# Merging two column-nesting subtractions into one, and four output planes of a unit into one addition

## The chip, the cores and the metric

The kernel runs on one core of one Trainium2 chip. The metric is the device time of one execution in microseconds (us). Engines are named as in the profile: PE (TensorE matmuls), PEld (weight loads), DVE (VectorE), ACT (ScalarE), POOL (GpSimd), SP (SyncE, which issues most DMAs).

## The reference, cut to what matters

```python
B, C, HW, E = 2, 512, 64, 1152           # bf16 in, bf16 out
def reference(x, t_emb, g1, be1, w1, w_emb, g2, be2, w2):
    h = conv3(_silu(gn(x, g1, be1)), w1)      # group norm, SiLU, 3x3 convolution
    emb = _silu(t_emb) @ w_emb
    h = h + emb.reshape(B, C, 1, 1)
    h = conv3(_silu(gn(h, g2, be2)), w2)
    return x + h
```

Both 3x3 convolutions run as a scheme that saves multiplications over rows: DVE makes combinations of input rows ("planes"), PE multiplies them, ACT moves the products out of PSUM, the memory that matmuls write to, with a scale (an "evacuation"), and DVE combines them into four output planes. From the second of the eight chunks on, columns are nested in the same way.

## The kernel before: the parts that matter

The work is cut into 32 "units" (8 chunks times 4 output channel tiles; the last unit has code of its own). The kernel holds nearly all of SBUF in one tile, the "arena", and places everything in it by hand:

```python
    VB = [o, o + 16640 + 2240 + 14848]        # column planes, two chunks
    Z = o + 16640 + 2240
    ...
    AB = [o, o + AF];  o += 2 * AF            # two input buffers; SiLU works in place in them
    YS = [o, o + YF];  o += 2 * YF            # two output buffers
    MB = o;            o += 4 * MS            # M: four planes of 512
    ...
    SD0 = Z + 10016                           # S: first layer
    O0 = [Z + 11552, Z + 12592, Z + 13632]    # o planes of the first layer
    SD1 = Z + 12768                           # S: second layer
    ar = pool.tile([P, NA], F16, name="ar")   # the arena
```

Every operation goes into the kernel's own planner with a modelled cost and with the exact set of elements that it reads and writes. The planner makes one order for each engine and then issues the program in that order. The tile framework, not the planner, decides afterwards which semaphores (signals that another engine or a DMA queue is done) each instruction waits for, from the program's order and from the access patterns.

```python
    def tt(out, a, b, op, name=""):
        pl.op("DVE", 0.075 + 0.000521 * out.n, lambda: nc.vector.tensor_tensor(out=out.ap, in0=a.ap, in1=b.ap, op=op),
              regs(a, b), regs(out), name)
```

A unit ends so, with `M(i)` at `MB + 512 i`:

```python
        tt(tw(SD, 512), M(0, 2), M(2, 2), AD, nm + "s")
        tt(M(0, 2), M(2, 2), M(0, 2), SB_, nm + "d")
        scal(se[0], M(2), M(1), 8.0, nm + "8")            # on ACT or DVE, by a table
        scal(se[1], M(3), M(1), 2.0, nm + "2")
        scal(se[2], A(SD + 1024, [[1, 512]]), A(SD + 512, [[1, 512]]), 4.0, nm + "4")
        yr = lambda r0: A(ys + r0 * RW, [[RW, 16], [33, 2], [1, 32]])
        tt(yr(0), A(MB, [[0, 2], [1, 512]]), A(MB + 1024, [[512, 2], [1, 512]]), AD, nm + "y")
        tt(yr(16), A(SD, [[0, 2], [1, 512]]), A(SD + 1024, [[-512, 2], [1, 512]]), AD, nm + "y")
```

The first addition (the "first" or M half below) reads M alone and needs two scaled planes, the second (the S half) reads S alone and needs one. The nesting (28 times) is four subtractions or additions over a small buffer X:

```python
        X = lambda i: A(xb + i, [[RW, 8 * nf], [1, 32]])
        for kind, (i, j, op) in enumerate(((32, 33, SB_), (1, 0, SB_), (33, 0, SB_), (33, 0, AD))):
            tt(A(vnest(c, ct, kind, 0), [[1, 256 * nf]]), X(i), X(j), op, nm)
```

## Time and profile before

| | before |
|---|---|
| median of the first 3 runs | 476.97 us (476.17 to 478.6) |
| span of the profiled run | 474.9 us |
| first matmul starts | 4.5 us |
| 2936 matmuls, each at the median spacing of its shape | 455.3 us |
| stalls of over 0.4 us between matmuls, in sum | 4.8 us |
| smaller excess between matmuls, in sum | 5.4 us |
| after the last matmul, itself counted at its median, to the end | 4.9 us |

The last five rows add up to the span. They are worked out from the start times of successive matmuls in the trace: the median distance is 222 ns for 512 columns and 109 ns for 256, and what exceeds the median of its shape is a stall. PE works at its pace nearly all the time.

The page of the kernel before: its line of busy times (with shares of the span and instruction counts), then busy tenths in 40 equal slices, and PE's granted clock in tenths.

```profile
PE 461.3 (97%) x2936; PEld 283.4 (60%) x2936; DVE 428.2 (90%) x847; ACT 371.9 (78%) x580; POOL 38.8 (8%) x66
...
PE   6998999899999999999999999999999999999995
...
DVE  1699999999999999988999999998999999996447
...
PEclk9998999999999999999999999999999999999999
```

Busy time of each engine in three stretches (the columns stand in the first line); PE is full in two of them.

```profile
core 0: us, PE busy (x) PEld busy (x) DVE busy (x) ACT busy (x) POOL busy (x), PEclk, DMA share, GB/s
80.00:100.00 20.00, 18.28 (x91) 8.76 (x90) 19.93 (x42) 17.87 (x40) 0.00 (x0) 1.00 0.43 142
180.00:200.00 20.00, 20.00 (x116) 11.14 (x114) 19.76 (x41) 14.66 (x33) 2.05 (x4) 1.00 0.62 201
290.00:310.00 20.00, 20.00 (x149) 14.35 (x148) 19.86 (x33) 16.84 (x20) 2.74 (x4) 1.00 0.67 171
```

DVE's groups by shape: count, busy us, mean ns of one, and idle time of DVE just before them with what ended it. The 15 additions of 2048 elements belong to another step (adding S onto M).

```profile
L328 DVE TENSOR_TENSOR ar<-ar 128x1024 f16<-128x1024 f16 x272 | 179.1, 692 | 11.4 <-ACT ar L351 10.7
...
L328 DVE TENSOR_TENSOR ar<-ar 128x512 f16<-128x512 f16 x78 | 31.1, 428 | 0.1
L328 DVE TENSOR_TENSOR ar<-ar 128x2048 f16<-128x2048 f16 x15 | 18.3, 1219 | 7.0 <-ACT ar L351 7.0
```

Who waited for whom, in us in total, times, and the longest:

```profile
ACT ar L351 <- DVE ar L328: 34.8, 35, 3.2
DVE ar L328 <- ACT ar L351: 24.2, 17, 3.8
...
PE psum L379 <- ACT ar L351: 1.7, 1, 1.7
...
PE psum L379 <- DVE fs L441: 1.2, 2, 0.9
```

PE itself waits little once it has started: beside these two entries there is one wait of 1.3 us for DVE, at 36 us.

### The profile page before, as it was taken

To read this page: it belongs to the slowest core of one execution; us is meant where nothing else is said; L and a number is where in the kernel's file an instruction comes from. 1 tells how busy PE (TensorE), PEld (TensorE's weight loads), DVE (VectorE), ACT (ScalarE), POOL (GpSimd) and SP (SyncE) were. 2 spreads that over 40 slices of the span, in tenths; PEclk is the share of its full clock that TensorE was granted. 3 is DMA by queue.
4 is the path that set the end of the run, shared out by engine and by line. 5 is a ranking of instruction groups with operands and counts; after the bars stand their busy time and mean duration, and the time that the engine had idled before them with its cause. 6 is when DMAs were issued, how large, how long until landed. Compare 5 with 4: busy or idle time off the path is not lost.

```text
span 474.9 us, 8229 instructions
## 1 busy us (share of the span) xinstructions
PE 461.3 (97%) x2936; PEld 283.4 (60%) x2936; DVE 428.2 (90%) x847; ACT 371.9 (78%) x580; POOL 38.8 (8%) x66
## 2 busy tenths in 40 slices
PE   6998999899999999999999999999999999999995
PEld 5753555455555545555555576666666666677783
DVE  1699999999999999988999999998999999996447
ACT  5878999899999777689988778768776788655452
POOL 4100000010000000100000001104011111111111
PEclk9998999999999999999999999999999999999999
DMA  8943566366252466664775886685778487366534
GB/s 326 373 160 109 159 203 190 96 223 219 94 172 77 179 187 201 184 235 159 253 259 197 290 273 214 166 225 135 200 184 227 100 251 190 117 128 138 112 46 90
DMA packets 40505, 87.18 MB, mean 184 GB/s; under 512 B 6416, under 2 KB 14480, under 8 KB 40464
## 3 DMA queue, kind: packets, MB, share of 16 engines
q1 hardware_dynamic: 35520, 77.60, 48.5%
q0 software_dynamic: 4656, 9.05, 12.3%
q8 instruction: 23, 0.38, 0.3%
q14 instruction: 18, 0.15, 0.1%
q10 hardware_dynamic: 288, 0.01, 0.0%
HBM read 62.25 MB, written 31.32 MB: 197 GB/s over the span
## 4 chain that ended last, share of the span: by engine, by line
PE 40%; DVE 24%; ACT 7%; issue 4%; POOL 0%; DVEq 0%; ACTq 0%; POOLq 0%
PE psum L379 40%; DVE ar L328 22%; ACT ar L351 7%; DVE ar L332 2%; POOL fs L450 0%; POOL ar L364 0%; DVEq L1176 0%; DVE fs L441 0%; DVE fs L914 0%; DVE fs L915 0%; DVE fs L452 0%; DVE fs L917 0%; DVE fs L921 0%; DVEq L328 0%; ACTq L351 0%
## 5 line engine op out<-in xcount | busy, mean ns | idle before, releaser
L379 PE MATMUL psum<-ar 128*128 128x512 f16 (+2 forms) x2729 | 443.7, 325 | 4.3 <-ACT ar L351 1.7
L328 DVE TENSOR_TENSOR ar<-ar 128x1024 f16<-128x1024 f16 (+5 forms) x689 | 404.0, 648 | 27.4 <-ACT ar L351 24.2
L379 PEld LDWEIGHTS <-ar 128*128 128x128 f16 (+1 forms) x2765 | 266.6, 98 | 175.2 <-issue 7.4
L351 ACT ACTIVATE ar<-psum 128x512 f16<-128x512 f32 (+2 forms) x224 | 156.5, 714 | 53.3 <-PE psum L379 44.7
L351 ACT ACTIVATE ar<-ar 128x512 f16<-128x512 f16 (+6 forms) x185 | 158.1, 890 | 31.2 <-DVE ar L328 30.2
L351 ACT ACTIVATE ar<-ar,fs 128x2112 f16<-128x2112 bf16 (+1 forms) x32 | 68.7, 2149 | 6.8 <-DVE fs L454 2.9
L364 POOL DMA_DIRECT2D out_dram<-ar x15 | 18.1, 1207 | 115.9 <-DVE ar L328 91.8
L332 DVE TENSOR_SCALAR ar<-ar 128x512 f16<-128x512 f16 (+2 forms) x73 | 26.4, 381 | 0.5 <-ACT ar L351 0.5
L379 PE MATMUL psum<-ar,ones_bf 128*128 128x260 bf16 x128 | 18.3, 284 | 4.5 <-DMA ar<-in_x_dram 4.5
L351 ACT ACTIVATION_READ_ACCUMULATOR ar<-psum 128x1 f32 x100 | 20.8, 208 | 0.0
L379 PEld LDWEIGHTS <-ones_bf 128*128 128x128 bf16 x128 | 12.6, 100 | 9.9 <-issue 3.2
L450 POOL TENSOR_TENSOR fs<-fs 128x1 f32<-128x1 f32 (+1 forms) x7 | 9.0, 1281 | 108.9 <-DVE fs L448 97.2
L368 POOL MEMSET ar<- 128x65 f16 (+5 forms) x28 | 4.4, 197 | 121.8 <-PE psum L379 29.5
L364 POOL DMA_DIRECT2D ar<-ar x4 | 3.7, 924 | 79.2 <-DVE ar L328 63.8
L351 ACT ACTIVATION_READ_ACCUMULATOR ar<-ar 128x1 f32 x36 | 7.1, 198 | 0.0
L441 DVE COPY fs<-psum 128x2 f32<-128x2 f32 (+1 forms) x7 | 1.1, 158 | 4.7 <-PE psum L379 4.7
L967 DVE SCALAR_TENSOR_TENSOR ar<-psum,ident 128x128 bf16<-128x128 f32 x4 | 1.2, 290 | 4.6 <-PE psum L379 4.6
L379 PEld LDWEIGHTS psum<-fs,ones_neg 128*128 128x128 f32 x36 | 4.6, 191 | 0.8 <-issue 0.3
L379 PE MATMUL psum<-fs,ones_neg 128*128 128x1 f32 (+3 forms) x36 | 4.7, 244 | 0.1
L452 DVE TENSOR_TENSOR fs<-fs 128x1 f32<-128x1 f32 (+1 forms) x7 | 1.1, 157 | 2.2 <-POOL fs L450 2.1
L415 ACT ACTIVATE s_sb<-tparm 128x18 bf16<-128x18 bf16 x1 | 0.2, 218 | 3.1 <-DMA tparm<-in_t_emb_dram 3.1
L410 ACT ACT_TABLE_LOAD x1 | 1.3, 1283 | 1.7 <-PEq L1165 1.7
(40 smaller groups left out, 17.9 us busy)
## 6 DMA issues: line engine op xcount, KB each, us to landing
ar<-in_w_dram SPq DMA_DIRECT2D x32, 384.0 KB, 3.9
ar<-in_x_dram SPq DMA_DIRECT2D x16, 552.5 KB, 3.9
h_scr<-ar SPq DMA_DIRECT2D x16, 520.0 KB, 3.4
ar<-h_scr SPq DMA_DIRECT2D x16, 520.0 KB, 3.9
out_dram<-in_x_dram SPq DMA_DIRECT2D x30, 260.0 KB, 4.7
out_dram<-ar POOLq DMA_DIRECT2D x15, 520.0 KB, 5.8
u_scr<-ar SPq DMA_DIRECT2D x16, 384.0 KB, 2.8
ar<-u_scr SPq DMA_DIRECT2D x4, 1536.0 KB, 7.0
```

What stands on the lines that cost most here:

```text
L328: pl.op("DVE", 0.075 + 0.000521 * out.n, lambda: nc.vector.tensor_tensor(out=out.ap, in0=a.ap, in1=b.ap, op=op), regs(a, b), regs(out), name)
L332: pl.op("DVE", cost or 0.075 + 0.00026 * out.n, lambda: nc.vector.tensor_scalar(out=out.ap, in0=a.ap, scalar1=s, scalar2=None, op0=ALU.mul ...
L351: lambda: nc.scalar.activation(out=out.ap, in_=a.ap, func=func, scale=sc, **kw), regs(*rr), regs(*ww), name)
L364: lambda: eng.dma_start(out=out, in_=in_, **kw), regs(*r), regs(*w), name, lat=3.2 if sw else None, after=after, sw=sw)
L368: pl.op("POOL" if eng == "gpsimd" else "DVE", 0.08 + 0.0005 * out.n, lambda: e.memset(out.ap, v), (), regs(out), name)
L379: nc.tensor.matmul(out.ap, lhsT=lhsT.ap, rhs=rhs.ap, start=st, stop=sp, skip_group_check=True)
L410: nc.scalar.activation(out=fs[:, WARM:WARM + 1], in_=fs[:, WARM + 1:WARM + 2], func=ACT.Silu)
L415: nc.scalar.activation(out=s_sb[:], in_=tparm[:], func=ACT.Silu)
L441: pl.op("DVE", 0.16, lambda: V.tensor_copy(out=F(tot, 2 * n).ap, in_=ps.ap), regs(ps), regs(F(tot, 2 * n)), name)
L450: pl.op("POOL", 0.85, lambda: nc.gpsimd.tensor_tensor(out=F(rs, n).ap, in0=N.ap, in1=F(NEGH, n).ap, op=ALU.pow), regs(N), regs(F(rs, n)), ...
L452: small(lambda: V.tensor_mul(out=S.ap, in0=F(rs, n).ap, in1=F(g, n).ap), [F(rs, n)], [S], name)
L967: pl.op("DVE", 0.3, lambda: nc.vector.scalar_tensor_tensor(out=j2.ap, in0=g.ap, scalar=1.0 / HW, in1=ident[:], op0=ALU.mult, op1=ALU.mult, ...
```

## The change

Intent: fewer DVE instructions for the same elements, 31 in the output additions (all units but the last) and 28 in the nesting, on an engine that is 90% busy. The two scaled planes in M change places so that one pattern can walk all four.

```diff
-        for kind, (i, j, op) in enumerate(((32, 33, SB_), (1, 0, SB_), (33, 0, SB_), (33, 0, AD))):
-            s0 = vnest(c, ct, kind, 0)
-            tt(A(s0, [[1, 256 * nf]]), X(i), X(j), op, nm)
+        X2 = lambda i, j: A(xb + i, [[j - i, 2], [RW, 8 * nf], [1, 32]])
+        tt(A(vnest(c, ct, 0, 0), [[1, 512 * nf]]), X2(32, 1), X2(33, 0), SB_, nm)
+        for kind, op in ((2, SB_), (3, AD)):
+            tt(A(vnest(c, ct, kind, 0), [[1, 256 * nf]]), X(33), X(0), op, nm)
...
-        scal(se[0], M(2), M(1), 8.0, nm + "8")
-        scal(se[1], M(3), M(1), 2.0, nm + "2")
+        scal(se[0], M(3), M(1), 8.0, nm + "8")
+        scal(se[1], M(2), M(1), 2.0, nm + "2")
...
-        yr = lambda r0: A(ys + r0 * RW, [[RW, 16], [33, 2], [1, 32]])
-        tt(yr(0), A(MB, [[0, 2], [1, 512]]), A(MB + 1024, [[512, 2], [1, 512]]), AD, nm + "y")
-        tt(yr(16), A(SD, [[0, 2], [1, 512]]), A(SD + 1024, [[-512, 2], [1, 512]]), AD, nm + "y")
+        tt(A(ys, [[RW, 32], [33, 2], [1, 32]]), A(MB, [[SD - MB, 2], [0, 2], [1, 512]]),
+           A(MB + 1536, [[SD - MB - 512, 2], [-512, 2], [1, 512]]), AD, nm + "y")
```

Between S and M lie the o planes of the first layer, the column planes of every second chunk (`VB[1]`), both input buffers `AB` and both output buffers `YS`.

## The prediction

> **What bounds the kernel now.** TensorE (PE). The page has PE busy 461.3 of 474.9 us (97%), VectorE (DVE) 428.2 (90%), ScalarE (ACT) 371.9. In the table of 20 us stretches PE is busy 20.00 of 20 in most stretches from 40 to 460 us. It is also at its own pace: start to start, successive 512-column matmuls stand 222 ns apart (median of 1247; 90th percentile 224) and 256-column ones 109 ns. With each matmul at its shape's median the 2936 matmuls need about 455.2 us. The rest of the span is 4.5 us before the first, 5.1 us after the last, and about 10 us of PE stalls: 1.4 us at 36 us (waits for DVE), 1.9 us at 90 us (waits for ACT), 1.0 us at 176 and 0.5 us at 289 us (wait for DVE in the second normalisation), and small ones, mostly before 41 us.
>
> DVE is full from 80 to 320 us (19 to 20 of 20), so it looks like a second limit, and the chain of waits that ended last runs along DVE from 114 to 177 us and from 229 to 289 us. But PE loses only about 1 us and 0.5 us where that chain enters PE. In the second layer the chain is PE alone: 1204 matmuls in 168.3 us. In the last unit it returns to DVE, and the change does not touch that unit's outputs.
>
> **What the change removes.** One DVE instruction in each of 31 units (two 1024-element additions become one of 2048), and one in each of 28 nested tiles (two 512-element subtractions become one of 1024 in 12 tiles; two of 1024 become one of 2048 in 16). Elements stay the same. Start to start the trace has 350 ns for a 512-element subtraction of this kind, 634 for one of 1024, 601 for a contiguous addition of 1024 and 1135 for 2048. So a merge saves about 2x601-1135 = 67 ns in a unit, 2x350-634 = 66 in a small tile and (an estimate) 70 to 130 in a large one: together 4 to 5 us, 1% of DVE's busy time. The Trainium skill (Vector Engine (DVE) Microarchitecture Reference, 5.2 Measured stream behaviour) gives about 75 ns per instruction; the trace's 67 agrees.
>
> **What it adds or moves.** The single output addition waits for all three scaled planes, where the first half needed two, and frees the intermediate planes about 0.6 us later. The nest needs nothing new. Zero and negative outer steps keep innermost steps of 1, so I expect the same rate per element. The planned order shifts: statistics matmuls of the second image move among the first units' matmuls, and one normalisation chain moves earlier.
>
> **On the critical path.** Only the part that shortens DVE-caused stalls counts: at most about 1.5 us at 176 and 289 us, likely half; the early stalls lie before any changed instruction. The 1.9 us at 90 us is an ACT matter that the new order may shrink or worsen by 1 to 2 us.
>
> **Prediction.** 475.8 us, 80% range 473.4 to 478.2. Faster by over 2%: 0.02; within 2%: 0.96; slower by over 2%: 0.02.
>
> **What would show the steps.** PE busy and matmul spacing unchanged; 59 fewer DVE instructions; merged additions near 1.22 us each, so DVE busy about 424 us; a little more DVE idle, mostly after 200 us; PE stalls near 176 and 289 us equal or shorter.
>
> **What would make it wrong.** Merged accesses at half rate: each output addition would take about 2.2 us, DVE busy would grow by over 30 us and PE would wait: 10 us or more slower. Or the new order putting a statistics matmul ahead of its data: some us of PE waiting before 100 us.

## The result, and the profile after

The changed kernel took 507.94 us (median of 4 runs, 506.35 to 510.5) against 476.83 us before (4 runs). The ratio is 1.065, with a 95% interval from 1.060 to 1.071: slower by over 6%. Ratios in this text are the mean time of one kernel's fast runs over that of the other's of the same rounds, so they are not quite the ratio of the medians quoted.

The same sum, for the profiled runs (us):

| | before | after |
|---|---|---|
| first matmul starts | 4.5 | 4.5 |
| matmuls at the median spacing of before | 455.3 | 455.3 |
| stalls of over 0.4 us | 4.8 | 27.4 |
| smaller excess | 5.4 | 11.6 |
| after the last matmul | 4.9 | 5.9 |
| span | 474.9 | 504.6 |

So 22.6 of the 29.7 us are new stalls of PE, and 6.2 are smaller excess; 5.0 of these are matmuls that run slowly after a stall, as shown below. The page of the changed kernel, the same lines as before:

```profile
PE 468.2 (93%) x2936; PEld 285.7 (57%) x2936; DVE 427.4 (85%) x788; ACT 370.5 (73%) x580; POOL 38.2 (8%) x66
...
PE   6989995999999939999999968999999998999995
...
DVE  1799959998996796887999899999989989985547
...
PEclk9999998999999988999999987999999999999999
```

DVE has 59 instructions fewer and is busy for 0.8 us less; it isn't slower, it stands idle more. Where it stands idle shows in the groups by shape:

```profile
L328 DVE TENSOR_TENSOR ar<-ar 128x1024 f16<-128x1024 f16 x190 | 126.8, 692 | 10.9 <-ACT ar L351 10.1
L328 DVE TENSOR_TENSOR ar<-ar 128x2048 f16<-128x2048 f16 x62 | 76.3, 1237 | 35.7 <-ACT ar L351 15.6 <-issue 9.9 <-DMA ar<-in_x_dram 8.1
...
L328 DVE TENSOR_TENSOR ar<-ar 128x512 f16<-128x512 f16 x54 | 21.3, 422 | 1.6 <-ACT ar L351 1.6
```

The 62 instructions of 2048 elements are 15 as before, 16 merged nests and 31 merged output additions. They take 1237 ns in the mean, so the full rate is kept: the half rate that the prediction named as its main danger did not come. But DVE now stands idle for 35.7 us ahead of this group. Sorted by operand shape in the trace, 28.9 us of it stand ahead of 21 of the 31 output additions (before: 0.6 us ahead of one). And part of it ended with a DMA from the input `x`, which no output addition needs.

The waits, the same pairs as before, with two new ones:

```profile
ACT ar L351 <- DVE ar L328: 69.7, 41, 5.8
...
DVE ar L328 <- ACT ar L351: 33.2, 28, 3.4
...
PE psum L379 <- ACT ar L351: 15.9, 7, 5.5
DVE ar L328 <- issue: 9.9, 5, 4.2
PE psum L379 <- DVE fs L441: 8.7, 2, 8.6
DVE ar L328 <- DMA ar<-in_x_dram: 8.1, 3, 4.6
```

ACT's waits for DVE doubled. One of PE's new waits, before and after (PE in order of time: start, us, what; in brackets the idle time before it). Before:

```profile
175.06 0.51 PE L379 MATMUL psum<-fs,ones_neg 128*128 128x8 f32 x4
175.42 0.81 PE L379 MATMUL psum<-ar 128*128 128x256 f16 x6
177.10 1.27 PE L379 MATMUL psum<-ar 128*128 128x512 f16 x5 [0.86 <-DVE fs L441]
```

After:

```profile
180.11 0.51 PE L379 MATMUL psum<-fs,ones_neg 128*128 128x8 f32 x4
180.47 1.03 PE L379 MATMUL psum<-ar 128*128 128x256 f16 x8
190.06 1.44 PE L379 MATMUL psum<-ar 128*128 128x512 f16 x3 [8.55 <-DVE fs L441]
```

The same 512-column matmul, after the small matmuls of the second normalisation, waited 0.86 us before and 8.55 us now, both for the DVE copy of the normalisation's sums (L441): DVE reached that copy late. What follows such a stall shows in the same stretches as before, in their number of matmuls and in the granted clock (the column after POOL):

```profile
core 0: us, PE busy (x) PEld busy (x) DVE busy (x) ACT busy (x) POOL busy (x), PEclk, DMA share, GB/s
80.00:100.00 20.00, 14.50 (x61) 6.45 (x61) 19.03 (x39) 16.49 (x33) 0.00 (x0) 0.83 0.47 149
180.00:200.00 20.00, 11.45 (x62) 6.19 (x60) 14.79 (x30) 11.79 (x24) 0.87 (x1) 0.83 0.46 129
290.00:310.00 20.00, 13.22 (x76) 8.47 (x74) 19.93 (x40) 15.36 (x21) 0.31 (x2) 0.74 0.80 283
```

After one stall of 5.7 us, which ends at 85.5 us, and after the one of 8.7 us, successive 512-column matmuls stand about 427 ns apart, 11 and 6 of them, in place of 222. The Trainium skill (TensorE: Matmul & The Clock Gate, "What's actually happening") says that PE falls to half its clock after an idle window of about 3.4 us and needs about as long a busy one to come back; its section "Wait — 56ns, not 53.3ns?" gives 426.7 ns for 512 columns at the half clock. This trace agrees with the 427 ns; slow running begins once after a stall of 2.8 us too (at 299 us). In the kernel before it is found only near 40 us, in seven matmuls, after the stall of 1.4 us at 36 us; its stalls of 0.5 to 1.9 us at 90, 176 and 289 us were not followed by it. So in these traces a stall well under 3.4 us can start it and need not.

What do the output additions wait for? That stands in the built programs, as the list of semaphores ahead of each instruction (DMAHW and DMASW are DMA queues; own numbers dropped). Three of the additions before, and the same units in the changed kernel (here "earlier" is the half that is issued first: S in units 4 and 9, M in unit 18):

```
before   unit 4   earlier: DMAHW6, DVE             later: DVE
before   unit 9   earlier: DMAHW7, ACT             later: DVE, ACT
before   unit 18  earlier: DMASW4, ACT             later: none
after    unit 4   DMAHW6, DMAHW7, DVE, ACT
after    unit 9   DMASW2, DMAHW3, DMAHW4, DVE, ACT, POOL
after    unit 18  DMASW4, DMAHW6, DMAHW7, DVE, ACT, POOL
```

POOL does nothing that an output addition of unit 9 could need: it writes zero rows in `AB` (and raises a power in the normalisation). This gave the theory.

**Theory T, false waits.** The merged access reaches from S to M across some 30,000 elements. The framework appears to take all that lies between as read. So the addition waits for loads, SiLU and evacuations that it doesn't need, and later writers of that stretch wait for it.

**Rival O, the order.** The planner got other entries, so it made another order on each engine, and that order is bad on the chip.

**Rival P, one instruction for two.** The single addition must wait for all three scaled planes, and holds M longer.

### The profile page after: what moved, and what is told of

Same layout as the page of the kernel before. It is cut to its first block, busy times and chain, and to the rows that moved or that the text cites. A ratio compares the mean times of both kernels' runs of the same rounds, so it can differ in the third digit from the quotient of the medians.

```text
span 504.6 us, 8130 instructions
## 1 busy us (share of the span) xinstructions
PE 468.2 (93%) x2936; PEld 285.7 (57%) x2936; DVE 427.4 (85%) x788; ACT 370.5 (73%) x580; POOL 38.2 (8%) x66
## 3 DMA queue, kind: packets, MB, share of 16 engines
q0 software_dynamic: 4656, 9.05, 11.6%
## 5 line engine op out<-in xcount | busy, mean ns | idle before, releaser
L379 PE MATMUL psum<-ar 128*128 128x512 f16 (+2 forms) x2729 | 450.3, 327 | 26.1 <-ACT ar L351 15.9
L328 DVE TENSOR_TENSOR ar<-ar 128x1024 f16<-128x1024 f16 (+6 forms) x630 | 401.9, 693 | 56.8 <-ACT ar L351 33.2
L351 ACT ACTIVATE ar<-ar 128x384 bf16<-128x384 bf16 (+6 forms) x185 | 158.5, 891 | 50.7 <-DVE ar L328 44.3
L364 POOL DMA_DIRECT2D ar<-ar x4 | 3.7, 923 | 85.5 <-ACT ar L351 64.6
L441 DVE COPY fs<-psum 128x2 f32<-128x2 f32 (+1 forms) x7 | 1.1, 159 | 4.7 <-PE psum L379 4.7
```

Source lines behind the costliest of these rows:

```text
L351: lambda: nc.scalar.activation(out=out.ap, in_=a.ap, func=func, scale=sc, **kw), regs(*rr), regs(*ww), name)
L364: lambda: eng.dma_start(out=out, in_=in_, **kw), regs(*r), regs(*w), name, lat=3.2 if sw else None, after=after, sw=sw)
L379: nc.tensor.matmul(out.ap, lhsT=lhsT.ap, rhs=rhs.ap, start=st, stop=sp, skip_group_check=True)
L441: pl.op("DVE", 0.16, lambda: V.tensor_copy(out=F(tot, 2 * n).ap, in_=ps.ap), regs(ps), regs(F(tot, 2 * n)), name)
```

## The experiments

Fifteen kernels ran, all with correct results, each against runs of the kernel before on the same chip (476.2 to 476.9 us in the median).

### y_near: the planes side by side, everything else the same

```diff
-    SD0 = Z + 10016
-    O0 = [Z + 11552, Z + 12592, Z + 13632]
-    SD1 = Z + 12768
+    O0 = [Z + 10016, Z + 11056, Z + 12096]
+    SD0 = SD1 = MB + 4 * MS          # S right behind M; the area Z is shorter by 1664
-    NF = 640
+    NF = 512                         # makes room; the kernel's own assertion says that these columns are unused
```

> The changed kernel with the planes M and SD laid side by side in the arena (nothing else lies between them); all instructions and their order on PE, DVE, ACT and SP are the same as in the changed kernel, as the built programs show; only the semaphore waits differ. Theory T (false waits): the merged output addition reads an access pattern that reaches from SD to M, and whatever lies between these two is taken for read, so the addition waits for loads and evacuations that it doesn't need, and they for it. T: 473 to 478 us, DVE idle ahead of the output additions under 4 us (28.9 in the changed kernel), no PE stall over 2 us after 100 us. Rival O (the planner's new order is bad on the chip): 505 to 511, stalls where they were. Rival P (one addition must wait for all three scaled planes, and holds M longer): 505 to 511 too.

Measured: 479.25 us (4 runs, 478.76 to 480.92), ratio to before 1.0056 (1.0025 to 1.0087). The loss is gone but for some 2.5 us, with the same instructions in the same order on PE, DVE, ACT and SP as in the 507.94 us. Ahead of the group of merged instructions DVE now idles 11.7 us in place of 35.7, and nothing but ACT ends it (mind that the 15 older additions of 2048 have about 6.7 of it; the output additions have 4.9):

```profile
L328 DVE TENSOR_TENSOR ar<-ar 128x1024 f16<-128x1024 f16 x190 | 127.1, 695 | 10.4 <-ACT ar L351 9.7
L328 DVE TENSOR_TENSOR ar<-ar 128x2048 f16<-128x2048 f16 x62 | 76.3, 1238 | 11.7 <-ACT ar L351 11.5
```

The stretches are full or nearly full again, at a clock of 1.00:

```profile
core 0: us, PE busy (x) PEld busy (x) DVE busy (x) ACT busy (x) POOL busy (x), PEclk, DMA share, GB/s
80.00:100.00 20.00, 18.65 (x93) 8.79 (x91) 19.85 (x39) 17.18 (x40) 0.00 (x0) 1.00 0.47 148
180.00:200.00 20.00, 20.00 (x116) 11.16 (x115) 19.86 (x39) 14.15 (x33) 1.18 (x3) 1.00 0.70 196
290.00:310.00 20.00, 18.68 (x134) 13.09 (x134) 19.91 (x32) 16.61 (x20) 3.32 (x5) 1.00 0.65 163
```

The waits in the built program are back to real ones: unit 4 waits for DMAHW6 and DVE, unit 9 for DVE and ACT, unit 18 for DMASW4, DVE and ACT. Matmul for matmul (the order on PE is the same), the changed kernel falls behind y_near by 7, 9 and 9 us near 82, 178 and 283 us, all in the first layer, and by some 4.5 us after 370 us. Rivals O and P, which both said 505 to 511, fall as the explanation of the 28 us. DVE's idle time ahead of the output additions fell by 24.0 us, the time by 28.7; how much of that comes from the additions' own waits, and how much from later writers that wait for them, was not separated. The expected 473 to 478 was missed by 1.3 us, and the 4 us of idle time by 0.9: something small is left. (No PE stall over 2 us after 100 us was expected; the longest is 1.8 us.)

### y_two_narrow: the changed plan, issued as two narrow instructions

The plan keeps its one entry of 2048 elements; only the issue differs:

```diff
-            nc.vector.tensor_tensor(out=<4 planes>, in0=<M and S>, in1=<M and S>, op=AD)
+            nc.vector.tensor_tensor(out=<planes 0, 1>, in0=<M>, in1=<M>, op=AD)
+            nc.vector.tensor_tensor(out=<planes 2, 3>, in0=<S>, in1=<S>, op=AD)
```

> The changed kernel, planned exactly as it is (one entry of 2048 elements in the plan), but the output addition issued as two instructions back to back, planes 0 and 1 from M, planes 2 and 3 from SD, as before. T: 474 to 479 us, no false waits, DVE pays about 67 ns more per unit. O: 505 to 511, for the order is that of the changed kernel. P: some 476 to 500, for the first half still sits where the plan put the whole.

Measured: 479.59 us (479.26 to 481.43), ratio 1.0065 (1.0033 to 1.0096), 0.6 us over the range. In the old arena, with the changed kernel's order, no wide access means no loss but for some 2.7 us, much as in y_near. Both issue in the order of the changed plan, so this rest belongs to that plan and not to the merged instruction. The 31 instructions that the merge saves are worth 0.34 us between the two medians, which is within the runs' scatter. The line of the additions in its page:

```profile
L840 DVE TENSOR_TENSOR ar<-ar 128x1024 f16<-128x1024 f16 x62 | 40.0, 688 | 4.9 <-ACT ar L351 4.9
```

### y_mid_wide: no merge, but one wide access

```diff
-            <one instruction for planes 0 to 3>
+            <plane 0: M alone>   512 elements
+            <planes 1 and 2: in0 = A(MB, [[SD - MB, 2], [1, 512]]), in1 = A(MB + 1024, [[SD - MB, 2], [1, 512]])>   1024
+            <plane 3: S alone>   512 elements
```

> The changed kernel's plan, but the output addition issued as three instructions: plane 0 (M alone), planes 1 and 2 together (an access that reaches from M to SD), plane 3 (SD alone). Not one instruction fewer than before, and M is no longer held by a single instruction. T: 500 to 515 us, the wide middle instruction alone brings the false waits back, and three instructions cost DVE about 0.13 us more per unit than one. O: 505 to 513. P: under 500. Together with the run with two narrow instructions it tells T from O.

Measured: 507.85 us (507.82 to 508.56), ratio 1.0654 (1.0621 to 1.0687): the whole loss, with three instructions in place of one. The merge isn't needed for it; the reach of the access is enough. The page's line of the three additions shows the loads of `x` again, which none of them needs:

```profile
L841 DVE TENSOR_TENSOR ar<-ar 128x512 f16<-128x512 f16 (+1 forms) x93 | 47.8, 514 | 24.3 <-DMA ar<-in_x_dram 8.6
```

### nest_only and y_only: each half of the change alone

> The kernel before with the merged nesting operation alone (output additions as before). T: within 1% of before, 472 to 481 us, for the merged access stays inside one small buffer; DVE loses 28 instructions and about 2 us of busy time. The plan comes out with quite another order on PE, so O leaves it open: anything from 475 to 510. P: as before, 475 to 478.

Measured: 476.97 us (476.42 to 477.71), ratio 1.0003 (0.9975 to 1.0030). The merged nest neither gains nor loses, although the planner made another order on PE for it.

> The other half of the change alone: output additions merged across M and SD in the old arena, nesting as before. T: 498 to 512 us, the whole loss, by whatever order the planner finds; with nest_only at 477.0 this splits the change.

Measured: 504.46 us (503.42 to 505.17), ratio 1.0589 (1.0571 to 1.0607). The output addition carries the loss, in yet another order.

### before_near: the layout alone

The kernel before with the arena of y_near.

> Control: the kernel before with the arena laid out as in y_near, all instructions in the same order. If the layout does nothing by itself: 475.5 to 478 us. If the remaining 0.6% of y_near came from the layout: 478 to 481.

Measured: 476.71 us (6 runs, 475.9 to 479.02), ratio 1.0009 (0.9984 to 1.0034). The layout does nothing by itself.

### wide_layer1 and wide_layer2: where the loss arises

The changed plan, with the wide addition in the units of one layer and two narrow ones in those of the other.

> The changed kernel's plan; the 16 units of the first layer issue the wide merged addition, the 15 of the second layer two narrow ones. By the stalls in the changed kernel's trace (some 23 us of PE stalls and slow restarts before 296 us, when the second layer begins), theory T expects most of the loss here: 494 to 504 us.

Measured: 503.50 us (502.82 to 504.34), ratio 1.0565 (1.0539 to 1.0591).

> The reverse: narrow pairs in the first layer, the wide merged addition in the 15 units of the second. T expects the smaller part: 482 to 492 us, and the two losses (against 479.6 with narrow pairs everywhere) to add up to about the 28 us of the changed kernel, within 6 us.

Measured: 485.46 us (483.54 to 486.07), ratio 1.0178 (1.0151 to 1.0206). Against the 479.59 us with narrow pairs everywhere the layers cost 23.9 and 5.9 us, 29.8 together, where the changed kernel has 28.4 more. The first layer bears most of it. In wide_layer1 the 31 instructions of 2048 on the first line are the older additions and the nests; the 16 wide output additions stand on a line of their own:

```profile
L328 DVE TENSOR_TENSOR ar<-ar 128x2048 f16<-128x2048 f16 x31 | 38.6, 1252 | 6.7 <-ACT ar L351 6.6
...
L843 DVE TENSOR_TENSOR ar<-ar 128x2048 f16<-128x2048 f16 x16 | 19.6, 1222 | 19.8 <-DMA ar<-in_x_dram 9.3 <-issue 7.2 <-ACT ar L351 1.8
```

Over 1.2 us of idle time for each in the mean (9 of the 16 wait), and most of it ended by loads of `x` or by what the profile can't name.

### ab_out and o0_out: what lies in between

One move in the arena each, in the changed kernel; the order of the instructions stays on PE, DVE, ACT and SP. To make room, ab_out also has `NF = 512`, as y_near does.

```diff
 ab_out
+    AB = [o, o + AF];  o += 4480      # in front of everything
     for j in range(CT): UREG.append(o) ...
-    AB = [o, o + AF];  o += 2 * AF
 o0_out
-    SD0 = Z + 10016;  O0 = [Z + 11552, Z + 12592, Z + 13632]
+    O0 = [Z + 10016, Z + 11056, Z + 12096];  SD0 = Z + 13136
```

> The changed kernel, same instructions in the same order on PE, DVE, ACT and SP, with one move in the arena: the two input buffers AB (loads, SiLU in place, zero rows) now lie outside the stretch between SD and M; the first layer's o planes, the column planes of every second chunk and the output buffers stay inside it. In the built program the additions' waits for loads and for the POOL zero rows are gone; those for ScalarE partly stay. T: most of the false waits are those on loads and SiLU of AB, so more than half of the 28 us comes back: 480 to 493 us.

Measured: 486.27 us (485.97 to 486.98), ratio 1.0211 (1.0196 to 1.0226).

> The reverse single move: o planes O0 of the first layer outside the stretch (SD0 and O0 change places), AB still inside; order the same as in the changed kernel on every engine. T with AB as the main cause: 498 to 508 us. If O0, whose evacuations free PSUM for PE, were the main cause: under 490, and ab_out near 500.

Measured: 506.58 us (505.69 to 508.35), ratio 1.0639 (1.0610 to 1.0669).

Taking the input buffers out of the stretch brings back 21.7 of the 31 us, although no output addition reads or writes them; taking out the o planes brings back 1.4, about the scatter. The merged group's line in ab_out:

```profile
L328 DVE TENSOR_TENSOR ar<-ar 128x2048 f16<-128x2048 f16 x62 | 76.2, 1235 | 18.2 <-ACT ar L351 11.9 <-DMA ar<-ar 5.7
```

and in o0_out:

```profile
L328 DVE TENSOR_TENSOR ar<-ar 128x2048 f16<-128x2048 f16 x62 | 76.3, 1237 | 36.2 <-ACT ar L351 17.7 <-issue 9.8 <-DMA ar<-in_x_dram 6.3
```

In ab_out no idle time of this group ends with a load of `x` any more; 5.7 us end with a DMA within the arena, which is the accumulating DMA into the column planes `VB[1]`, and `VB[1]` still lies between S and M. In the built program its queues are the only foreign DMA queues left (DMASW1 to DMASW3, in units 8 to 10, while the fourth chunk is prepared). So the false waits go with the buffer that is moved out, as T says. What `VB[1]`, `YS` and the rest cost each was not tried.

### merged_old_order, and four runs to explain it

Can the merged kernel beat both? This run takes both merges and the layout of y_near, but plans on the old entries. It was meant to put a merged instruction where the later of its two halves stood. In the built program that is so for the output addition in the 9 units where the S half came later; in the other 22 it stands at most one place behind where the S half stood. Its order on PE and SP is that of the kernel before.

```diff
+        pl.pairs.append((q - 1, q))     # issue the two entries as one, at the place of the second
```

> Both merges, with M and SD side by side, but planned on the old entries: the order on PE and SP is exactly that of the kernel before, and a merged instruction stands where the later of its two halves stood. If the span of the access is the whole cost and the new plan's order accounts for the 0.6% that remained in y_near: 474.5 to 477.5 us, at or a little under before. If merging itself costs something: 478 to 481 as y_near.

Measured: 487.86 us (6 runs, 486.85 to 488.74), ratio 1.0237 (1.0215 to 1.0260). That was a miss: no false waits, and 11 us lost all the same. The output additions (first line; the nests are left out, the older additions stand below) follow 11.9 us of idle time, 11.5 of which ACT ended:

```profile
L865 DVE TENSOR_TENSOR ar<-ar 128x2048 f16<-128x2048 f16 x31 | 38.0, 1224 | 11.9 <-ACT ar L374 11.5
...
L351 DVE TENSOR_TENSOR ar<-ar 128x2048 f16<-128x2048 f16 x15 | 18.3, 1219 | 5.4 <-ACT ar L374 5.4
```

First guess (merged_late): the half that came first used to run while ACT scaled the last plane, and a later place for the whole would heal it.

```diff
+        pl.late[q] = 0.7                # us by which the plan lets the merged addition slip
```

> merged_old_order again (487.9 us, 11.7 us of DVE idle ahead of the output additions, some 0.7 us each in 17 units: the first half no longer fills the wait for ScalarE's scaling), with the merged addition let slip 0.7 us in the plan so that independent DVE work goes ahead of it. If that wait is what merged_old_order lost: DVE idle ahead of the additions under 5 us and 475.5 to 481 us. If the loss came from holding M longer instead: 487 or more.

Measured: 487.01 us (486.03 to 487.69), with 9.5 us of idle time still ahead of the output additions. The edit did not remove the wait that it was to remove, so it neither confirms the guess nor rules it out. Three more runs undid one part each; the first is nest_old_order.

> merged_old_order with the output additions as before: only the nesting merged, at the place of the later half, order of before on PE, ACT and SP. If the output addition loses the 11 us: 475 to 478 us. If the nest loses them: 485 to 489.

Measured: 477.58 us (477.20 to 479.27), ratio 1.0027 (0.9994 to 1.0060). Not the nest. Next, y_old_order.

> merged_old_order with the nesting as before: only the output addition merged, at the place of its later half, M and SD side by side. If the output addition loses them: 484 to 490 us, with DVE idle ahead of the additions of 8 us or more. Otherwise 475 to 479.

Measured: 488.50 us (486.60 to 488.87), ratio 1.0241 (1.0212 to 1.0271). The output addition. Last, halves_late.

> y_old_order with the addition issued as the two narrow instructions of before, back to back at the place of the later half. If the place is what costs (the first half no longer runs while ScalarE scales the last plane, and M comes free later): within 3 us of y_old_order, 484 to 491. If the merged instruction costs (it alone waits for the third plane): 475 to 480, for the first half can still start before the third plane is scaled.

Measured: 488.16 us (487.46 to 489.34), ratio 1.0245 (1.0219 to 1.0271). Two narrow instructions, moved together, cost as much as one. That doesn't tell the place from the instruction, though: the run issues the M half first, and all the idle time stands ahead of M halves in units where the S half had come first. There the S half used to run while ACT still scaled planes of M; now it stands behind the wait of the M half, as it does inside the merged instruction. A run with the S half in front was not made. In this run DVE's idle time ahead of its 272 additions of 1024 elements is 21.8 us, against 11.4 before:

```profile
L351 DVE TENSOR_TENSOR ar<-ar 128x1024 f16<-128x1024 f16 x272 | 178.6, 694 | 21.8 <-ACT ar L374 20.8
```

By operand shape, 10.9 us of that stand ahead of 17 M halves, where before there were 0.6 us ahead of one; ahead of the S halves there is none in either kernel. Matmul for matmul (PE's order is that of before), halves_late falls behind near 70, 105, 177, 290 and 394 to 411 us. One thing besides moved: by the built program ten successive instructions of ACT, near 90 us, come in another order. Between 80 and 120 us PE loses about 1 us net, so most of the loss arises elsewhere. By which later instruction it reaches PE is open. What is shown is that in the old order binding the two halves together costs 11 to 12 us (what rival P feared, though not the cause of the 28 us), and that the planner, when told of the merged entry, finds an order that loses only some 2.5 us (y_near).

No version beat the kernel before: the best with any part of the change are nest_only and nest_old_order, both level with it.

## Why the prediction was wrong, point by point

- **"What bounds the kernel now": right, and it stays right.** The matmuls need the same 455.3 us in both kernels. All that is lost lies in stalls, slow matmuls after them, and 1 us at the end.
- **"What the change removes": right in kind, at the lower end in size, and worth nothing.** 59 instructions went; merged additions took about 1.22 us as predicted. Start to start a merged addition of y_near takes 1135 ns against two of 602, and a large nest 1201 against two of 634, so each saves 67 to 69 ns (the large nest was guessed at 70 to 130): about 4 us in all, an estimate from these medians, where 4 to 5 were said. DVE's busy time, though, fell by only 2.6 us (428.2 to 425.6). No run shows a gain from it: nest_only stands at 1.0003, and one instruction in place of two in the same order was worth 0.34 us (479.25 against 479.59), within the scatter.
- **"What it adds or moves": this is the step that failed.** The prediction said that "the single output addition waits for all three scaled planes, where the first half needed two", and took that for the whole list. It asked what data the addition needs, and not what the built program makes it wait for. The changed program was at hand and lists, for unit 9, four semaphores that the same addition doesn't wait for in y_near: three DMA queues and POOL. Those waits cost 28 to 29 us: they vanish with S beside M at the same order (y_near), return without any merge when one access is wide (y_mid_wide), and shrink by 22 us when `AB` alone is moved out (ab_out).
- **Within that step, "frees the intermediate planes about 0.6 us later" was set down as harmless.** In the old order, binding the two halves together costs 11 to 12 us (y_old_order, halves_late). The prediction thought of the M half as the one that goes first; in 22 of the 31 units it was the S half, and the waits came there. In the changed kernel's own order what remains after the false waits are gone is about 2.5 us, 0.6%.
- **"On the critical path": wrong in its logic.** The prediction counted only the gain in PE's present stalls, and saw no way for DVE to make new ones. DVE is 19 to 20 of 20 us busy in every stretch from 80 to 320 us but one (17.0 from 200 to 220, which the prediction passed over), and PE follows close behind it: where DVE's idle time ahead of the output additions rose from 0.6 us to 11.9 (merged_old_order) and 28.9 (the changed kernel), the time rose by 11 and 31 us.
- **"What would make it wrong": both named dangers missed.** Half rate didn't come (1237 ns in the mean for 2048 elements). The order with statistics matmuls among the first units was not it either: y_near has that order, and its stall near 80 us is 1.2 us where the changed kernel has 5.7.

## What to carry to other kernels

When two accesses are merged into one pattern with a far step, look at what lies in memory between its ends, and compare the semaphore waits of the built program before and after, not only the data that the instruction needs: a framework that orders by access patterns may take the whole stretch as touched. If the merge is wanted, first lay the operands side by side. And where one engine follows close behind another that is full, moving an instruction later or giving it a wait can cost about the whole wait, as here, while removing an instruction's fixed cost may give nothing.

## What the Trainium skill lacked or had wrong

- No page that was read says how the waits of an instruction come about from an access pattern that spans memory it doesn't touch. Here one such pattern per unit cost 28.7 us of 508 (507.94 against 479.25 us, same instructions, same order on four engines). It belongs beside VectorE: DVE Perf Modes, "🎯 Rules for kernel authors", whose row on chained operations says "Minimize op *count*, not sems". The row speaks of chained DVE operations; here a lower count with more semaphores to wait for lost 6.5%.
- Vector Engine (DVE) Microarchitecture Reference, 5.2 Measured stream behaviour: about 75 ns per instruction, for streams of 4-byte elements unless stated otherwise. Here, with f16, 67 ns for an output addition (2x601-1135 ns start to start before). Saving 59 of them changed the time by nothing that the runs could show.
- TensorE: Matmul & The Clock Gate has 512-column matmuls about 216 ns apart at full clock; here the median is 222 ns over 1247 of them. Its half-clock figure of 427 ns is what the trace shows after the stalls of 5.7 and 8.7 us; compared with before, slow running cost 5.0 us on top of the stalls, a term that the prediction didn't have. The page ties the fall to an idle window of about 3.4 us; here it also came after stalls of 1.4 us (before, at 36 us) and 2.8 us (changed kernel, at 296 us).
